# Attention rows as two 64-row matmuls, with heads regrouped at the load

## The chip, the cores and the metric

The kernel runs on one core of one Trainium2 chip. The metric is the device time of one execution in microseconds (us); the time before is the median of three runs. A profile is taken of one further execution, and its own time is given beside it.

## What is computed

A Nystrom attention with 32 landmarks per head is followed by a normalised MLP with a residual. There are 8 batches of 8 heads, 576 positions and 64 features per head.

```python
q_lm = q.reshape(B, H, 32, 18, D).mean(axis=3); k_lm = ...      # landmarks
A  = softmax(scale * q @ k_lm.T)      # 576 x 32 per head
Bm = softmax(scale * q_lm @ k_lm.T)   # 32 x 32
C  = softmax(scale * q_lm @ k.T)      # 32 x 576
Z  = Bm.T / (norms);  six times: Z = 2 * Z - Z @ Bm @ Z
attn = A @ Z @ C @ v                  # per head
x  = attn with heads side by side     # 8 x 576 x 512
xn = (x - mean) / sqrt(var + 1e-6) * g_ln
out = x + relu(xn @ w_ch1) @ w_ch2    # 512 -> 2048 -> 512
```

## The kernel before

**Units.** Four heads make a unit `u`, so a batch has two units (`U` = 2). Within a unit the four heads' 32 landmarks fill the 128 partitions. Batches 0 and 1 are handled one by one by `attention(b)`; batches 2 to 7 by `attention2` in four sets: (2), (3, 4), (5, 6) and (7).

**Loads.** All loads stand in one queue, that of SP, in program order. Batches 0 and 1 use `load` (L80), one copy of 128 partitions per tensor and unit. Batches 2 to 7 use `load_seg` (L100): k and q and the even v units are one copy of 128 rows of 4608 bytes (576 KB as the profile counts it). The odd v units are `turned`: two copies of 64 rows with the halves exchanged. Tiles come from the pool `stage` with six buffers, so a load waits until POOL has cast the tile loaded six places before it. SP's queue also holds the stores of results (`store`, L749) and the transposing copies of `xn` into `xnT` (L732).

**Casts and landmarks.** `Coming` (L497) holds the parts of a set in the order k, q, v and hands out loads, casts and jobs; `prepare` (L917) calls it between steps. POOL casts each load to fp16 (`nat`, `natv`) and, for most q tiles, adds up the 18 rows of a landmark (`asum`, `s`). DVE transposes the tiles (`xT`) and finishes the landmarks (`lmk`, `lmq`).

**Rows.** `rows_of` (L467) makes one block of at most 128 output positions at a time. Per unit it multiplies `ea` (the unit's exponentials, 128 landmark rows by up to 128 positions) with `zcbd`, a block-diagonal 128 x 260 tile: four heads of 64 columns plus four mask columns that give the sum of each softmax. The products go to `psy`, in one bank per unit, DVE takes reciprocals (`rcpd`) and scales (`xblk`). `zcbd` is made by one masked DVE product per unit.

**MLP stream.** `mlp()` is a generator of matmuls in nine groups of four blocks: `psh` (first layer, needs the four `xnT` blocks of the group), then `pso` (second layer). `fill(n)` puts n of its steps into TensorE's queue between the steps of the attention. The order on every engine is thus fixed when the program is built. `hT` (ACT) and `ot` (DVE) empty the three banks of the pool `psM`, which `psh`, `pso`, the transposes and dummy tiles share. In groups 2 and later the `xnT` blocks come by the transposing copies.

**Prologue.** `warm(n, cols)` issues dummy matmuls on zeros into a `psM` tile named `idle`. `turn_tile` transposes tiles of batches 0 and 1 on TensorE, `sums` adds landmarks up there.

**Exchange of halves.** In `scores` and in the products of `attention2` the odd unit of a pair uses column positions shifted by 64, so that its results come out with exchanged halves. Before, v of odd units is loaded exchanged to fit, and a second mask `mask4t` serves these units.

Of the kernel before, what the change touches and what calls it, by code (L numbers as in the profile page):

```python
# [9 lines left out]
FP16 = mybir.dt.float16  # L10
FP32 = mybir.dt.float32
UINT32 = mybir.dt.uint32
AF = mybir.ActivationFunctionType
ALU = mybir.AluOpType
AX = mybir.AxisListType

P = 128
# [3 lines left out]
def kernel(  # L21
# [10 lines left out]
    nc = tc.nc  # L32

    B, H, S, D = q.shape
# [5 lines left out]
    SEG = S // LM  # L40
    KCH = DM // P
    MCH = HID // P
    U = H // 4
    NJ = 9
# [7 lines left out]
        name=nc.get_next_instruction_name(), act_func_set_id=6, ins=[], outs=[]))  # L52

    const = ctx.enter_context(tc.tile_pool(name="const", bufs=1))
# [5 lines left out]
    keep = tc.keep_in_program_order  # L60
# [8 lines left out]
    dve, pool, scalar = Ordered(nc.vector), Ordered(nc.gpsimd), Ordered(nc.scalar)  # L69
    act = scalar.activation  # L70

    def MM(o, l, r, rb=0, cb=0, start=True, stop=True, skip=False):
        keep(nc.tensor.matmul(o, l, r, start=start, stop=stop, tile_position=(rb, cb),  # L73
                              skip_group_check=(skip or cb != 0)))
# [5 lines left out]
    def load(src, b, u, queue):  # L80
        t = stage.tile([P, 2, NJ, D], FP32, name="stg", tag="stg")
        keep(queue.dma_start(
            out=t[:],
            in_=src[b, 4 * u:4 * u + 4].rearrange("(r e) (t j) d -> (e t) r j d", e=2, j=NJ)))
        return t

    raw = {0: {}, 1: {}}
# [11 lines left out]

    def load_seg(src, b, u, queue, turned=False):  # L100
        t = stage.tile([P, SEG, D], FP32, name="stg", tag="stg")
        rows = src[b, 4 * u:4 * u + 4].rearrange("h (l j) d -> (h l) j d", j=SEG)
        for o, i_ in ((0, 64), (64, 0)) if turned else ((0, 0),):
            n = 64 if turned else P
            keep(queue.dma_start(out=t[ds(o, n), :, :], in_=rows[ds(i_, n), :, :]))
        return t


# [34 lines left out]
    mask4 = const.tile([P, 4], FP32, name="mask4")  # L143
# [10 lines left out]
                            base=63, pattern=[[64, 2]], channel_multiplier=-1)  # L154


    mask4t = const.tile([P, 4], FP32, name="mask4t")
    nc.gpsimd.tensor_copy(out=mask4t[:, 0:2], in_=mask4[:, 2:4])
    nc.gpsimd.tensor_copy(out=mask4t[:, 2:4], in_=mask4[:, 0:2])

    eps_ln = const.tile([P, 1], FP32, name="eps_ln")
    nc.vector.memset(eps_ln[:], 1e-6)
# [3 lines left out]
    NZ = 6  # L166
    natv_buf = []
    for i in range(NV):
        t = const.tile([P, H // 2, NJ, D + 1], FP16, name=f"natv{i}")
        nc.gpsimd.memset(t[:, :, :, D:D + 1], 1.0)  # L170
        natv_buf.append(t)
    zcbd_buf = []
    for i in range(NZ):
        zcbd_buf.append(const.tile([P, 4 * (D + 1)], FP16, name=f"zcbd{i}"))

    def zc_of(i):
        return zcbd_buf[i][:, ds(4 if i % 2 == 0 else 0, 4 * D)].rearrange("p (h d) -> p h d", d=D)

    cast_v(0)
    bones = const.tile([P, 4, 32], FP16, name="bones")
    for u in range(U):
        for nm in ("q", "k"):
            cast_qk(0, u, nm, dve)
        if u == 0:

            dve.tensor_copy(out=bones[:], in_=mask4[:, :, None].broadcast_to([P, 4, 32]))
            for i, t in enumerate(zcbd_buf):
                dve.tensor_copy(out=t[:, ds(0 if i % 2 == 0 else 4 * D, 4)],  # L190
                                in_=(mask4t if i in (3, 5) else mask4)[:])


    load_qk(1)
# [54 lines left out]
    def warm(n, cols):  # L249
        idle = psM.tile([P, 512], FP32, name="idle", tag="pm")  # L250
        for _ in range(n):
            MM(idle[:, 0:cols], zeros[:, 0:P], zeros[:, 0:cols])
# [27 lines left out]
    def turn_tile(b, w, nm):  # L280
        i = 0 if nm == "q" else 1
        if b == 1:
            if not i and w == 0:
                pss = ps1.tile([P, 2, U, 64], FP32, name="pss", tag="p1")
                nat_pss[b, 0], nat_pss[b, 1] = pss[:, 0, :, :], pss[:, 1, :, :]
            turn_part(w, nm, 0)
            turn_part(w, nm, 1)
            return None
        if w == 0:
            nat_pss[b, i] = psM.tile([P, U, 64], FP32, name="pss" + nm, tag="pm")  # L290
        n16 = nat_tiles[b, nm, w]
        t = aprep.tile([P, NJ, P], FP16, name="xT", tag="xT" + nm, bufs=5 if nm == "q" else 4)
        early_xT[b, nm, w] = t
        last = (w, i) == (U - 1, 1)
        pst = ps2.tile([P, NJ, P], FP16, name="pst", tag="p2")
        if last:
            sums(b, w, i, n16)
        for j in range(NJ):
            TR(pst[:, j, :], n16[:, j, :, :].rearrange("p r d -> p (r d)"), ident16[:])
        if not last:  # L300
            scalar.copy(t[:], pst[:])
            sums(b, w, i, n16)
        return t, pst

    def attention(b):
        W, first = U, b == 0
# [5 lines left out]
        def p2(shape, dtype, name):  # L312
# [4 lines left out]
            out=qbd[:],  # L317
            in0=nat_pss[b, 0][:].rearrange("p u (e l) -> p (u e) l", e=2)[:, :, None, :]
            .broadcast_to([P, W * 2, 2, LM]),
            in1=mask2[:, None, :, None].broadcast_to([P, W * 2, 2, LM]), op=ALU.mult)  # L320
# [8 lines left out]
        for w in range(W):  # L329
            for h in range(4):  # L330
                r, e = divmod(h, 2)
# [8 lines left out]
        for w in range(W):  # L340
# [5 lines left out]
            t = aexp.tile([P, NJ, 64], FP16, name="ect", tag="e")  # L346
# [7 lines left out]
        ea = []  # L354
# [52 lines left out]
        pszc = p1([P, W, D], "pszc")  # L407
        for w in range(W):
            for h in range(4):
                sl = ds(32 * h, 32)  # L410
                MM(pszc[sl, w, :], st[sl, w, LM:], cv[sl, w, :], rb=32 * h, cb=32 * h)
        zcbd = []
        for w in range(W):
            dve.tensor_tensor(
                out=zc_of(w), in0=pszc[:, w, None, :].broadcast_to([P, 4, D]),
                in1=mask4[:, :, None].broadcast_to([P, 4, D]), op=ALU.mult)
            zcbd.append(zcbd_buf[w])
        yield "zc"

        yield from rows_of((b,), ea, zcbd)  # L420

    def softmax_of(psb, W):
        rsum = asm.tile([P, W], FP32, name="rsum", tag="rsum")
# [41 lines left out]


    def rows_of(bs, ea, zcbd):  # L467
        for i, b in enumerate(bs):
            t0 = 0
            while t0 < S:  # L470
                j, pb = divmod(b * S + t0, P)
                n = min(P - pb, S - t0)
                rows = ds(pb, n)
                xb = x_of(j)
                psy = ps2.tile([P, U * 512], FP32, name="psy", tag="p2")
                for u in range(U):
                    MM(psy[rows, ds(508 - 256 if u == 0 else 512, 4 * (D + 1))],
                       ea[U * i + u][:, ds(t0, n)], zcbd[U * i + u][:], cb=pb)
                rcpd = asm.tile([P, U * 4], FP32, name="rcpd", tag="rcpd")
                dve.reciprocal(  # L480
                    out=rcpd[rows, :].rearrange("s (u h) -> s u h", u=U),
                    in_=psy[rows, ds(252, 520)].rearrange("s (a x) -> s a x", x=4)[:, 0::129, :])
                if pb == 0:
                    rowsum[j] = mstat.tile([P, 1], FP32, name="rowsum", tag="rowsum")
                dve.scalar_tensor_tensor(
                    out=xb[rows, :].rearrange("s (h e) -> s h e", e=D),
                    in0=psy[rows, ds(256, 512)].rearrange("s (h e) -> s h e", e=D), scalar=1.0,
                    in1=rcpd[rows, :, None].broadcast_to([n, 8, D]),
                    op0=ALU.mult, op1=ALU.mult, accum_out=rowsum[j][rows, :])
                t0 += n  # L490
                if pb + n == P:
                    block_done(j)
                yield "rows"
# [3 lines left out]
    class Coming:  # L497
# [28 lines left out]
        def load(self, i, queue=nc.sync):  # L526
            nm, w = self.parts[i]
            b, u = self.units[w]
            self.stg[i] = load_seg({"q": q, "k": k, "v": v}[nm], b, u, queue,
                                   turned=(nm == "v" and u % 2 == 1))  # L530


        def cast(self, i):
# [66 lines left out]
    def attention2(bs, c):  # L600
# [63 lines left out]
                    ea.append(e)  # L664
            yield
        pszc = ps2.tile([P, 2, 512], FP32, name="pszc", tag="p2")
        zcbd = []
        for w in range(W):
            for h in range(4):
                sl = ds(32 * h, 32)  # L670
                cb = 32 * ((h + 2 * (w % 2)) % 4)
                MM(pszc[ds(cb, 32), w % 2, ds(D * (w // 2), D)], st[sl, w, LM:], cv[sl, w, :],
                   rb=32 * h, cb=cb)
        for w in range(W):
            dve.tensor_tensor(
                out=zc_of(2 + w),
                in0=pszc[:, w % 2, None, ds(D * (w // 2), D)].broadcast_to([P, 4, D]),
                in1=(mask4t if w % 2 else mask4)[:, :, None].broadcast_to([P, 4, D]),
                op=ALU.mult)
            zcbd.append(zcbd_buf[2 + w])  # L680
        yield

        yield from rows_of(bs, ea, zcbd)

    ln_ready = {0}
    rowsum, variances, rstds, xn_of = {}, {}, {}, {}
# [165 lines left out]
    def fill(n):  # L852
        for _ in range(n):
            if not next(stream, False):
                return
# [8 lines left out]
    for w, nm in [(w, nm) for w in range(U) for nm in ("q", "k")]:  # L864
        last_tile = turn_tile(0, w, nm)
        if (w, nm) == (1, "q"):
            next(a0)
        warm(2, 384)
    next(a0)
    warm(1, 512)  # L870
    next(a0)
    warm(1, 512)
    scaled_by_pe()
# [14 lines left out]
    turn_tile(1, 1, "q")  # L888
    sums(1, 0, 0, nat_tiles[1, "q", 0])
    sums(1, 0, 1, nat_tiles[1, "k", 0])  # L890
    warm(1, 384)
    load_v(1)
    fill(1)
    turn_tile(1, 1, "k")
    sums(1, 1, 0, nat_tiles[1, "q", 1])
    fill(1)
    next(a0)
    warm(1, 256)
    fill(2)
    next(a0)  # L900
    fill(4)
# [95 lines left out]
```

## Time and profile before

| | |
|---|---|
| median of 3 runs | 329.57 us (328.02 to 329.58) |
| the profiled execution's own time | 330.85 us |
| its span, first to last instruction | 329.1 us |
| mean TensorE clock granted | 0.992 |
| TensorE busy | 315.4 us in 3668 matmuls |
| HBM read | 36.70 MB |

The page gives busy time by engine, then the span in 40 slices of 8.2 us (a digit is tenths busy, and a line gives the GB/s moved by the 16 DMA engines), then the chain of work that ended last, then groups of instructions and DMA issues with their time to landing. A timeline line reads: start, length, engine, code line, operation, written tile <- read tiles, rows*columns of the array used, shape, count, and in brackets the idle time before and who ended it. The end of a matmul is modelled, so distances between starts say more than lengths. A line of a stretch gives for each engine the busy us and the count, then the mean clock, the DMA engines' mean busy share and GB/s.

### The profile page before, as it was taken

The page shows a single profiled execution, that of the slowest core. Times are in us where ns is not written, and L with a number is a line of the kernel's source. Part 1 is how long each engine was busy: PE and PEld are TensorE (multiplying, and loading weights), DVE is VectorE, ACT ScalarE, POOL GpSimd, SP SyncE. Part 2 cuts the span into 40 slices and gives each one's busy share as a digit, 9 for nine tenths or more (in the row PEclk, how much of TensorE's full clock was granted, in tenths as well). Part 3 has the DMA queues.
Part 4 walks back from the last instruction along what each step waited for, and adds up shares of the span by engine and source line. Part 5 has one row for each costly group of instructions (what it writes and reads, how often), then busy time and mean ns, then how long its engine had stood idle before and what let it go on. Part 6 is the DMA issues. An engine that isn't in the chain of part 4 may idle for free.

```text
span 329.1 us, 8722 instructions
## 1 busy us (share of the span) xinstructions
PE 315.4 (96%) x3668; PEld 160.1 (49%) x3668; DVE 142.3 (43%) x368; ACT 149.3 (45%) x295; POOL 125.4 (38%) x193
## 2 busy tenths in 40 slices
PE   8789999799978999999999999999999999999994
PEld 8557755344433444544544454544444444444443
DVE  2667239767972368767142356411441120010012
ACT  3376853367630572586214574463068107305600
POOL 2489879958899651397400022100043000000000
PEclk9999999799999999999999999999999999999998
DMA  7999999879997696541024022320241124032023
GB/s 278 394 385 385 386 405 270 323 229 244 327 236 268 165 336 198 112 100 33 4 66 83 16 35 64 82 50 2 64 97 32 32 64 98 0 75 57 0 55 72
DMA packets 34095, 50.37 MB, mean 153 GB/s; under 512 B 17540, under 2 KB 17800, under 8 KB 34056
## 3 DMA queue, kind: packets, MB, share of 16 engines
q1 hardware_dynamic: 34056, 49.82, 52.1%
q8 instruction: 28, 0.46, 0.6%
q14 instruction: 11, 0.09, 0.1%
HBM read 36.70 MB, written 9.44 MB: 140 GB/s over the span
## 4 chain that ended last, share of the span: by engine, by line
PE 89%; DVE 4%; DMA 2%; ACT 1%; issue 1%; SPq 0%
PE psh L73 39%; PE pso L73 37%; PE pscv L73 3%; PE psy L73 3%; DMA stg<-in_k_dram 2%; PE psn L73 2%; DVE xblk L67 1%; ACT xT L67 1%; PE psec L73 1%; PE psea L73 1%; DVE xT L67 1%; DVE lmk L67 1%; DVE ot L67 1%; PE idle L73 0%; PE psb L73 0%
## 5 line engine op out<-in xcount | busy, mean ns | idle before, releaser
L73 PE MATMUL pso<-w,hT 128*128 128x512 f16 (+1 forms) x592 | 135.3, 376 | 0.0
L73 PE MATMUL psh<-xnT,w 128*128 128x512 f16 (+1 forms) x640 | 135.2, 358 | 0.1
L67 ACT ACTIVATE hT<-psh 128x512 f16<-128x512 f32 x144 | 84.6, 598 | 82.1 <-PE psh L73 81.6
L73 PEld LDWEIGHTS <-w 128*128 128x128 f16 x640 | 59.0, 98 | 56.3 <-issue 1.1
L73 PEld LDWEIGHTS <-hT 128*128 128x128 f16 x592 | 56.2, 98 | 58.0 <-issue 2.1
L67 DVE SCALAR_TENSOR_TENSOR ot<-pso,rstd,xblk 128x512 f32<-128x512 f32 (+1 forms) x37 | 27.1, 732 | 88.3 <-PE pso L73 87.9
L67 ACT ACTIVATE junk<-xblk,negm 128x512 f16<-128x512 f32 x36 | 26.0, 721 | 35.5 <-POOL negm L67 35.2
L67 POOL TENSOR_SCALAR negm<-rowsum 128x1 f32<-128x1 f32 x28 | 5.3, 190 | 94.2 <-DVE xblk L67 93.2
L67 POOL CAST nat<-stg 128x1152 f16<-128x1152 f32 x28 | 31.5, 1144 | 6.7 <-DMA stg<-in_q_dram 5.2
L67 DVE SCALAR_TENSOR_TENSOR xblk<-psy,rcpd 128x512 f32<-128x512 f32 (+1 forms) x40 | 27.6, 691 | 2.2
L67 DVE SCALAR_TENSOR_TENSOR st<-st,psn 128x128 f16<-128x128 f16 (+2 forms) x36 | 11.3, 315 | 30.6 <-PE psn L73 30.5
L67 POOL CAST natv<-stg 128x1152 f16<-128x1152 f32 x16 | 18.1, 1147 | 12.9 <-DMA stg<-in_v_dram 10.3
L67 DVE STREAM_TRANSPOSE xT<-nat 128x576 uint32<-128x576 uint32 x24 | 18.4, 767 | 6.1 <-PE psea L73 6.1
L67 POOL TENSOR_SCALAR xn<-xblk,negm 128x512 f16<-128x512 f32 x28 | 19.1, 692 | 0.8
L73 PE MATMUL psy<-zcbd,ea 128*128 128x260 f16 (+1 forms) x80 | 15.6, 276 | 0.6 <-DVE zcbd L67 0.5
L67 DVE TENSOR_REDUCE lmk<-xT 128x64 f16<-128x1152 f16 x12 | 16.1, 1342 | 0.0
L67 POOL TENSOR_TENSOR asum<-asum 128x256 f32<-128x256 f32 (+2 forms) x30 | 15.0, 500 | 2.4
L67 DVE RECIPROCAL rcpd<-psy 128x8 f32<-128x8 f32 (+1 forms) x40 | 8.0, 201 | 17.1 <-PE psy L73 16.9
L67 ACT ACTIVATE ea<-psea 128x576 f16<-128x576 f32 x12 | 7.1, 647 | 15.4 <-PE psea L73 15.4
L67 POOL TENSOR_TENSOR asum<-nat 128x576 f32<-128x576 f16 x10 | 12.8, 1276 | 0.8
L73 PEld LDWEIGHTS <-st 32*32 32x32 f16 x448 | 5.6, 89 | 15.3 <-issue 9.5
L73 PE MATMUL pscv<-natv,ecT 32*32 32x65 f16 x864 | 9.8, 195 | 3.0 <-issue 3.0
(98 smaller groups left out, 205.0 us busy)
## 6 DMA issues: line engine op xcount, KB each, us to landing
stg<-in_q_dram SPq DMA_DIRECT2D x16, 576.0 KB, 7.0
stg<-in_k_dram SPq DMA_DIRECT2D x16, 576.0 KB, 8.5
out_dram<-ot SPq DMA_DIRECT2D x70, 128.0 KB, 2.3
wstg<-in_moe_w_ch_dram SPq DMA_DIRECT2D x16, 512.0 KB, 6.9
stg<-in_v_dram SPq DMA_DIRECT2D x10, 576.0 KB, 6.6
stg<-in_v_dram SPq DMA_DIRECT2D x12, 288.0 KB, 8.9
xnT<-xn SPq DMA_TRANSPOSE x28, 2.7
out_dram<-ot SPq DMA_DIRECT2D x4, 64.0 KB, 2.0
```

Source lines behind the costliest of these rows:

```text
L67: return lambda *args, **kw: keep(getattr(self.engine, op)(*args, **kw))
L73: keep(nc.tensor.matmul(o, l, r, start=start, stop=stop, tile_position=(rb, cb), skip_group_check=(skip or cb != 0)))
```

## The change

Heads are regrouped: unit `u` now holds heads 2u, 2u+1, 4+2u and 5+2u, so that the lower 64 partitions belong to heads of the first half of the row and the upper 64 to the second half. `load` keeps one copy of 128 partitions. `load_seg` always makes two copies of 64 partitions; the exchange moves from v to q and k of odd units. The rows matmul of each unit is split into two with 64 rows of the array each: half `f` of both units goes to one bank. `zcbd` becomes one tile per batch with two heads per partition half (130 columns), made by one masked product for both units. In the prologue some dummy matmuls go and one turn moves behind other work.

```diff
 def load(src, b, u, queue):
-        in_=src[b, 4 * u:4 * u + 4].rearrange("(r e) (t j) d -> (e t) r j d", e=2, j=NJ)))
+        in_=src[b].rearrange("(r w e) (t j) d -> w (e t) r j d", r=2, e=2, j=NJ)[u]))
 def load_seg(src, b, u, queue, turned=False):
     t = stage.tile([P, SEG, D], FP32, name="stg", tag="stg")
-    rows = src[b, 4 * u:4 * u + 4].rearrange("h (l j) d -> (h l) j d", j=SEG)
-    for o, i_ in ((0, 64), (64, 0)) if turned else ((0, 0),):
-        n = 64 if turned else P
-        keep(queue.dma_start(out=t[ds(o, n), :, :], in_=rows[ds(i_, n), :, :]))
+    rows = src[b].rearrange("(r w e) (l j) d -> w r (e l) j d", r=2, e=2, j=SEG)[u]
+    for half in range(2):
+        keep(queue.dma_start(out=t[ts(half, 64), :, :], in_=rows[half ^ turned]))
...
-    mask4t = const.tile([P, 4], FP32, name="mask4t")
-    nc.gpsimd.tensor_copy(out=mask4t[:, 0:2], in_=mask4[:, 2:4])
-    nc.gpsimd.tensor_copy(out=mask4t[:, 2:4], in_=mask4[:, 0:2])
+    masks = const.tile([P, 2], FP32, name="masks")
+    nc.gpsimd.tensor_tensor(out=masks[:], in0=mask4[:, 0:2], in1=mask4[:, 2:4], op=ALU.add)
...
-        zcbd_buf.append(const.tile([P, 4 * (D + 1)], FP16, name=f"zcbd{i}"))
+    zcbd_buf = [const.tile([P, 2, 2, D + 1], FP16, name=f"zcbd{i}") for i in range(NZ // 2)]
...
-            for i, t in enumerate(zcbd_buf):
-                dve.tensor_copy(out=t[:, ds(0 if i % 2 == 0 else 4 * D, 4)],
-                                in_=(mask4t if i in (3, 5) else mask4)[:])
+            for t in zcbd_buf:
+                dve.tensor_copy(out=t[:, :, :, D],
+                                in_=masks[:, None, :].broadcast_to([P, 2, 2]))
...
-        for w in range(W):
-            dve.tensor_tensor(
-                out=zc_of(w), in0=pszc[:, w, None, :].broadcast_to([P, 4, D]),
-                in1=mask4[:, :, None].broadcast_to([P, 4, D]), op=ALU.mult)
+        masked(zcbd_buf[0], pszc[:])
+    def masked(out, zc):
+        dve.tensor_tensor(out=out[:, :, :, 0:D], in0=zc[:, :, None, :].broadcast_to([P, 2, 2, D]),
+                          in1=masks[:, None, :, None].broadcast_to([P, 2, 2, D]), op=ALU.mult)
...
 def rows_of(bs, ea, zcbd):
+    first = 512 - 4 * (D + 1)
     for u in range(U):
-        MM(psy[rows, ds(508 - 256 if u == 0 else 512, 4 * (D + 1))],
-           ea[U * i + u][:, ds(t0, n)], zcbd[U * i + u][:], cb=pb)
+        for f in range(2):
+            half = ts(f, 64)
+            MM(psy[rows, ds(first + 2 * (D + 1) * (2 * f + u), 2 * (D + 1))],
+               ea[U * i + u][half, ds(t0, n)],
+               zcbd[i][half, u, :, :].rearrange("p a e -> p (a e)"), rb=64 * f, cb=pb)
...
-                               turned=(nm == "v" and u % 2 == 1))
+                               turned=int(nm != "v" and u % 2 == 1))
...
-        warm(2, 384)
+        if (w, nm) != (U - 1, "k"):
+            warm(2, 384)
     next(a0)
-    warm(1, 512)
...
-    warm(1, 384)
     load_v(1)
     fill(1)
-    turn_tile(1, 1, "k")
     sums(1, 1, 0, nat_tiles[1, "q", 1])
     fill(1)
+    turn_tile(1, 1, "k")
     next(a0)
-    warm(1, 256)
     fill(2)
```

In `attention2` the masked products of a pair of units become one in the same way. DVE reads `psy` at a stride of 65 for `rcpd` and `xblk`.

More of the change, by code (lines that the diff above doesn't have):

```diff
@@ L171 @@
         natv_buf.append(t)
-    zcbd_buf = []
-    for i in range(NZ):
-        zcbd_buf.append(const.tile([P, 4 * (D + 1)], FP16, name=f"zcbd{i}"))
-    def zc_of(i):
-        return zcbd_buf[i][:, ds(4 if i % 2 == 0 else 0, 4 * D)].rearrange("p (h d) -> p h d", d=D)
+    zcbd_buf = [const.tile([P, 2, 2, D + 1], FP16, name=f"zcbd{i}") for i in range(NZ // 2)]
     cast_v(0)
@@ L411, in attention @@
                 MM(pszc[sl, w, :], st[sl, w, LM:], cv[sl, w, :], rb=32 * h, cb=32 * h)
-        zcbd = []
-        for w in range(W):
-            dve.tensor_tensor(
-                out=zc_of(w), in0=pszc[:, w, None, :].broadcast_to([P, 4, D]),
-                in1=mask4[:, :, None].broadcast_to([P, 4, D]), op=ALU.mult)
-            zcbd.append(zcbd_buf[w])
+        masked(zcbd_buf[0], pszc[:])
         yield "zc"
-        yield from rows_of((b,), ea, zcbd)
+        yield from rows_of((b,), ea, zcbd_buf[0:1])
+    def masked(out, zc):
+        dve.tensor_tensor(out=out[:, :, :, 0:D], in0=zc[:, :, None, :].broadcast_to([P, 2, 2, D]),
+                          in1=masks[:, None, :, None].broadcast_to([P, 2, 2, D]), op=ALU.mult)
     def softmax_of(psb, W):
@@ L476, in rows_of @@
                 for u in range(U):
-                    MM(psy[rows, ds(508 - 256 if u == 0 else 512, 4 * (D + 1))],
-                       ea[U * i + u][:, ds(t0, n)], zcbd[U * i + u][:], cb=pb)
+                    for f in range(2):
+                        half = ts(f, 64)
+                        MM(psy[rows, ds(first + 2 * (D + 1) * (2 * f + u), 2 * (D + 1))],
+                           ea[U * i + u][half, ds(t0, n)],
+                           zcbd[i][half, u, :, :].rearrange("p a e -> p (a e)"),
+                           rb=64 * f, cb=pb)
+                heads = psy[rows, ds(first, 8 * (D + 1))].rearrange("s (h x) -> s h x", x=D + 1)
                 rcpd = asm.tile([P, U * 4], FP32, name="rcpd", tag="rcpd")
-                dve.reciprocal(
-                    out=rcpd[rows, :].rearrange("s (u h) -> s u h", u=U),
-                    in_=psy[rows, ds(252, 520)].rearrange("s (a x) -> s a x", x=4)[:, 0::129, :])
+                dve.reciprocal(out=rcpd[rows, :], in_=heads[:, :, D])
                 if pb == 0:
@@ L486, in rows_of @@
                     out=xb[rows, :].rearrange("s (h e) -> s h e", e=D),
-                    in0=psy[rows, ds(256, 512)].rearrange("s (h e) -> s h e", e=D), scalar=1.0,
+                    in0=heads[:, :, 0:D], scalar=1.0,
                     in1=rcpd[rows, :, None].broadcast_to([n, 8, D]),
@@ L666, in attention2 @@
         pszc = ps2.tile([P, 2, 512], FP32, name="pszc", tag="p2")
-        zcbd = []
         for w in range(W):
@@ L673, in attention2 @@
                    rb=32 * h, cb=cb)
[L674 to L680, printed above, removed]
+        for y in range(W // 2):
+            masked(zcbd_buf[1 + y], pszc[:, :, ts(y, D)])
         yield
-        yield from rows_of(bs, ea, zcbd)
+        yield from rows_of(bs, ea, zcbd_buf[1:])
     ln_ready = {0}
```

## The prediction

> **What bounds the kernel now.** I read the page's shares and chain first, then its DMA rows, then busy time by stretch, then TensorE's timeline at the places where something else could end last.
>
> ```profile
> PE 315.4 (96%) x3668; PEld 160.1 (49%) x3668; DVE 142.3 (43%) x368; ACT 149.3 (45%) x295; POOL 125.4 (38%) x193
> ...
> DMA  7999999879997696541024022320241124032023
> GB/s 278 394 385 385 386 405 270 323 229 244 327 236 268 165 336 198 112 100 33 4 66 83 16 35 64 82 50 2 64 97 32 32 64 98 0 75 57 0 55 72
> ...
> PE 89%; DVE 4%; DMA 2%; ACT 1%; issue 1%; SPq 0%
> ...
> stg<-in_v_dram SPq DMA_DIRECT2D x10, 576.0 KB, 6.6
> stg<-in_v_dram SPq DMA_DIRECT2D x12, 288.0 KB, 8.9
> ```
>
> TensorE carries 89% of the chain. But for the first 130 us (16 slices of 8.2 us) the DMA engines are nearly full too, and a 288 KB load takes longer to land than a 576 KB one. The stretches say why:
>
> ```profile
> core 0: us, PE busy (x) PEld busy (x) DVE busy (x) ACT busy (x) POOL busy (x), PEclk, DMA share, GB/s
> 44.00:49.00 5.00, 5.00 (x70) 2.49 (x69) 2.54 (x9) 1.28 (x3) 3.70 (x5) 1.00 1.02 410
> 50.00:55.00 5.00, 5.00 (x30) 2.66 (x29) 4.85 (x13) 1.44 (x2) 4.52 (x8) 1.00 1.03 228
> 77.00:80.00 3.00, 3.00 (x30) 1.17 (x28) 2.40 (x5) 2.29 (x7) 2.69 (x6) 1.00 0.99 218
> 116.00:119.00 3.00, 3.00 (x60) 1.42 (x58) 2.94 (x6) 2.60 (x6) 2.09 (x3) 1.00 1.04 230
> 120.00:126.00 6.00, 6.00 (x88) 2.63 (x88) 4.26 (x9) 3.55 (x7) 1.59 (x2) 1.00 1.02 409
> ```
>
> The engines are busy all the time (share 1.0), yet move 410 GB/s while whole 128-row loads pass and 218 to 230 while the `turned` v loads pass, which are two copies of 64 rows each.
>
> ```profile
> 46.55 0.81 PE L73 MATMUL pso<-w,hT 128*128 128x512 f16 x3
> 47.29 0.41 PE L73 MATMUL psy<-zcbd,ea 128*64 128x260 f16 x2
> 47.63 1.47 PE L73 MATMUL pso<-w,hT 128*128 128x512 f16 x6
> 48.94 0.39 PE L73 MATMUL psy<-zcbd,ea 128*128 128x260 f16 x2
> 49.16 0.59 PE L73 MATMUL pso<-w,hT 128*128 128x512 f16 x2
> ...
> 59.44 0.22 PE L73 MATMUL psb<-lmk,lmq 32*32 32x32 f16 x8 [1.67 <-DVE lmq L67]
> ...
> 106.40 0.81 PE L73 MATMUL psh<-xnT,w 128*128 128x512 f16 x3
> ...
> 141.00 0.38 PE L73 MATMUL psh<-xnT,w 128*128 128x512 f16 x1
> ```
>
> A full-array rows step costs 0.22 us (48.94 to 49.16), with no gap: six `pso` at 0.216 from 47.63 end at 48.93. A step in 64 columns costs 0.43: `pso` ends at 46.55 + 3 x 0.216 = 47.20 and resumes at 47.63. Two places wait on loads: 59.44, where TensorE waits for q's landmarks, and the starts of MLP groups 2 and 3 (106.40, 141.00), which need the four transposed `xnT` blocks. Those transposes stand in SP's queue behind the loads.
>
> [...] The trace agrees for column tiles (0.09 us in, about 0.10 out). It has no fp16 tile of 64 rows by 128 columns; the nearest, the one 4-row by 128-column product (`psg`, 13.22), starts 0.10 after the 512-column product ahead of it (12.90 + 0.22) has streamed. [...] The trace agrees after the wait at 59.44: the mean clock from 60 to 71 us is 0.84, 0.16 x 11 = 1.7 us of work lost.
>
> **Loads.** `load_seg` now issues two 64-row copies for every k, q and v unit of batches 2 to 7: 36 loads, of which 6 were split before. SP issues 30 more copies at 0.33 to 0.58 us, at most 17 us over 85; SP's waits for buffers (12.6 us on `natv`, 6.5 on `nat`) and for stores (99.9 on `ot`) cover that. The data path has none. A load is 590 kB: at 410 GB/s 1.44 us, at 226 (mean of 228, 218, 230) 2.61, so 1.17 more. Batches 0 and 1 (`load`) keep 128 rows and 2304-byte runs: nothing.
>
> I follow the queue in SP's order. The first such load (issued 38.84, landing 7.0 later) moves from 44.4. Six stage buffers keep up to 16 us of loads in flight, more than POOL's longest job (cast 1.14 and sums 3.6), so I take the queue as never empty.
> - Set 0 (batch 2): k lands at 47.0, 49.6, q at 52.2, 54.8. POOL casts and sums the first q until 52.2 + 4.7 = 56.9, the second until about 61.6. Before, that was 58.1 and DVE's last `lmq` started at 59.97. TensorE's wait at 59.44 grows by about 1.7.
> - Group 2 needs `xnT` of block 11. Ahead of it: 24 loads (62.6), four blocks of stores (0.65 each by bytes: 2.6), four transposes (estimate 1.2 each from SP's median issue 1.23: 4.8). 44.4 + 70.0 = 114.4, against 106.40: TensorE 8.0 late. On the way DVE's in-order queue blocks: its transpose of the first k of the next set (the 19th load) ran at 93.48, and that k now lands at about 98. Behind it on DVE stand `st`, `ecT` and `ot`; `ot` frees the `psM` banks that the next `pso` products want. This wait is part of the 8.0, not beside it.
> - Group 3 needs block 15: all 36 loads (94.0), ten blocks of stores (6.5), eight transposes (9.6): 154.5, landing about 155. TensorE would be there at 114.4 + 34.6 + 1.7 (cold clock) = 150.7. It starts **14.0 late**.
> - Afterwards nothing is loaded and TensorE is dense. The wait just ended costs one cold window: **+1.7**.
>
> **Rows on TensorE.** 32 full steps: two pairs of 130 columns at about 0.06 each if the halves overlap, plus 0.09 in, 0.10 out and 0.01 for the first weights: 0.32 instead of 0.22, +0.10 each. Eight 64-row steps already pay the switch: 0.43 to 0.33. In all +3.2 - 0.8 = +2.4. Unmeasured, so bounded: no drain for row tiles gives -0.10 x 40 = -4.0; halves that don't overlap 0.21 x 32 = +6.7. I take the drain, since every other mode change in the trace pays it. What falls before group 3 hides in the waits above; after it lie 12 full steps and three 64-row ones: +1.2 - 0.3 = **+0.9** (-1.5 to +2.5).
>
> **Mask products.** 16 DVE products of 0.42 become 8: 3.4 us of DVE, which idles 87.9 us on `pso` anyway. Only in the prologue does TensorE wait for the second (psy at 20.27): -0.4. Reads of `psy` at stride 65 have no row; I keep 0.69 us, and a tenth more on four steps between 49 and 59 would be 0.3, inside the wait.
>
> **Prologue order.** Dummy products of 1920 columns go (0.8 us, partly in waits), and they held `psM` buffers; k's turn moves behind block 1's transposes, so `psh` at 25.39 comes up to 0.9 earlier, until POOL's weight casts (0.69 each, the twelfth done at 29.79) meet it: about -0.5. Three small fills (0.15 each) and one POOL copy go, under input landings up to 9.8. All of this is lost again in the longer wait at 59. The clock could drop without the dummies: at most 1.7, hidden likewise. 160 more TensorE instructions less 10 shift the two "issue" pauses of the chain (1.66 and 1.34): -3 to +3, before group 2, hidden too.
>
> **Sum.** 14.0 + 1.7 + 0.9 = 16.6. The profiled execution is 330.85 (span 329.1), so 347.4; it stands 1.3 above the median of 329.57, hence **346.1**.
>
> **Rivals.** *A, the loads stay hidden:* engines fall out of step, so that one half's tail and the next half's head use both sides. At 2.2 us a load block 15 lands near 140 and block 11 near 105: nothing waits but 59.44. Then +2.4 rows, +0.6 wait, -0.9 prologue: about 332 (330 to 335). For it: the page's 8.9 us is a latency. Against it: in all three stretches the rate stayed near half for as long as halves were in flight, also beside whole loads (50 to 55). *B, faster:* a row tile of full width needs no drain; rows give -4.0, prologue -0.9: 325. It decides only if the switch costs under 0.05 us each way and a load takes under 2.2 us; the place is each `psy` step between two `pso` or `psh` products. For it: a row tile leaves all columns in use. Against it: `psg` above, and the load rates. *C, the change doesn't do what it says:* the two halves' products run one after another. Rows then cost +6.7, of which 12 x 0.21 = 2.5 after group 3 shows: 348.
>
> **Chances and range.** Forecast with C 0.83, A 0.11 (a third within 0.5%), B 0.06. Within 0.5% (1.6 us) is about what a measurement of this kernel can't tell from no change. Faster 0.06, same 0.04, slower 0.90. At 2.4 us a load the sum is +9 (338); at 2.9 (what 590 kB takes at 203, a tenth below the lowest stretch shown) +27 (357). The range takes these and A's upper edge: 334 to 357.
>
> **What would show it.** Right: the load rows read 288 KB throughout; GB/s near 225 to about 150 us; `psh` groups 2 and 3 start near 114 and 155 after idle TensorE; `lmq` later at 59; a rows step of 0.32. Wrong: GB/s over 300 with only halves in flight, group 3 starting by 143, or `psy` steps of 0.12.

## The result, and the profile after

| | before | after |
|---|---|---|
| median | 329.57 us (328.02 to 329.67, 4 runs) | 347.94 us (345.07 to 348.48, 4 runs) |
| ratio | | 1.055 (95% interval 1.049 to 1.062) |
| the profiled execution's own time, its span | 330.85, 329.1 us | 347.65, 345.9 us |
| mean TensorE clock granted | 0.992 | 0.975 |

The changed kernel is 18 us slower; 346.1 was forecast. The lines of its page that answer to those shown of before:

```profile
PE 321.1 (93%) x3743; PEld 155.5 (45%) x3743; DVE 140.5 (41%) x357; ACT 150.0 (43%) x295; POOL 126.0 (36%) x192
...
DMA  7999999999999999993012302250124034022022
GB/s 275 391 387 385 373 229 239 261 292 213 213 208 162 281 205 213 220 214 67 2 28 56 75 17 45 63 83 12 32 64 87 2 83 99 2 61 62 2 56 68
...
PE 75%; DMA 12%; POOL 7%; issue 3%; SPq 1%; DVE 1%; ACT 0%; POOLq 0%
...
stg<-in_k_dram SPq DMA_DIRECT2D x24, 288.0 KB, 10.6
stg<-in_q_dram SPq DMA_DIRECT2D x24, 288.0 KB, 9.9
stg<-in_v_dram SPq DMA_DIRECT2D x24, 288.0 KB, 8.3
```

The DMA digits are 9 up to slice 18 (155 us; before up to about 130), while the rate falls from 373 to 229 GB/s in slice 6, from 43 us, where the first halved loads arrive, and then lies between 162 and 292, mostly near 215, to the end of the loads. TensorE's share of the chain fell from 89% to 75%, and DMA took 12%. All 72 copies of batches 2 to 7 are of 288 KB now. TensorE's timeline at the places that the prediction named:

```profile
62.16 0.22 PE L73 MATMUL psb<-lmk,lmq 32*32 32x32 f16 x8 [1.25 <-DVE lmq L67]
63.34 0.21 PE L73 MATMUL psb<-lmk,lmq 32*32 32x32 f16 x6 [0.96 <-DVE lmq L67]
...
110.40 0.42 PE L73 MATMUL pscv<-natv,ecT 32*32 32x65 f16 x31 [5.44 <-issue]
110.75 4.06 PE L73 MATMUL pso<-w,hT 128*128 128x512 f16 x11
114.65 0.81 PE L73 MATMUL psh<-xnT,w 128*128 128x512 f16 x3
...
154.66 0.47 PE L73 MATMUL psh<-xnT,w 128*128 128x512 f16 x1 [2.08 <-DMA xnT<-xn]
```

Group 2 starts at 114.65 (before 106.40), but nothing at its start waits for `xnT`: the wait is 5.44 us of "issue" (time in which the engine waited for nothing that the profile shows) ahead of 110.40, in the middle of 72 equal products, and the 11 `pso` after it take 3.90 us where 2.38 would do (0.216 each). Group 3 starts at 154.66 and does wait for the transposing copy. By stretches (the last three columns are clock, DMA share and GB/s):

```profile
core 0: us, PE busy (x) PEld busy (x) DVE busy (x) ACT busy (x) POOL busy (x), PEclk, DMA share, GB/s
50.00:55.00 5.00, 5.00 (x32) 1.89 (x32) 3.88 (x12) 1.44 (x2) 2.30 (x2) 1.00 1.03 236
85.00:95.00 10.00, 10.00 (x61) 3.89 (x58) 9.70 (x24) 5.01 (x10) 9.01 (x15) 1.00 1.04 219
107.00:114.00 7.00, 3.60 (x39) 1.44 (x40) 0.00 (x0) 0.00 (x0) 6.60 (x10) 0.51 1.15 195
155.00:158.00 3.00, 3.00 (x11) 0.87 (x10) 0.91 (x3) 1.11 (x3) 1.33 (x3) 0.50 0.68 147
```

In the stretch over the first wait the clock is 0.51 on average, after the second 0.50: half.

### The profile page after: what moved, and what is told of

It is laid out like the page before. It is cut to its first block, busy times and chain, and to the rows that moved or that the text cites. A ratio compares the mean times of both kernels' runs of the same rounds, so it can differ in the third digit from the quotient of the medians.

```text
span 345.9 us, 8904 instructions
## 1 busy us (share of the span) xinstructions
PE 321.1 (93%) x3743; PEld 155.5 (45%) x3743; DVE 140.5 (41%) x357; ACT 150.0 (43%) x295; POOL 126.0 (36%) x192
## 4 chain that ended last, share of the span: by engine, by line
PE 75%; DMA 12%; POOL 7%; issue 3%; SPq 1%; DVE 1%; ACT 0%; POOLq 0%
PE psh L73 34%; PE pso L73 33%; DMA wstg<-in_moe_w_ch_dram 4%; POOL w L67 4%; DMA stg<-in_q_dram 3%; PE pscv L73 2%; DMA stg<-in_v_dram 2%; PE psy L73 2%; POOL asum L67 2%; PE psn L73 1%; DMA xnT<-xn 1%; POOL natv L67 1%; PE psea L73 1%; PE psec L73 1%; POOL nat L67 1%
## 5 line engine op out<-in xcount | busy, mean ns | idle before, releaser
L73 PE MATMUL psh<-xnT,w 128*128 128x512 f16 (+1 forms) x640 | 136.8, 361 | 2.3 <-DMA xnT<-xn 2.1
L73 PEld LDWEIGHTS <-hT 128*128 128x128 f16 x592 | 54.5, 98 | 59.8 <-issue 1.9
L73 PEld LDWEIGHTS <-ea 64*128 64x128 f16 (+1 forms) x160 | 4.9, 97 | 18.5 <-issue 14.1
```

## The experiments

Each experiment is named for the kernel that it starts from: those called after_ edit the changed kernel, those called before_ the kernel before; rows_only edits the changed kernel too. The starts of the MLP groups (from the timelines of the profiled executions), as differences to before, show where each kernel loses its time. A profiled execution need not lie at its kernel's median: that of before took 330.85 us, 1.3 above it, that of before_halves 341.22, 1.7 below, so the table is for the places of the losses and the medians for their sizes.

| us later than before | group 1 | group 2 | group 3 | last product |
|---|---|---|---|---|
| changed kernel | +4.0 | +8.3 | +13.7 | +16.3 |
| before_halves | +3.0 | +9.9 | +9.9 | +9.9 |
| before_far | +3.6 | +8.7 | +11.1 | +11.1 |
| after_near | +4.0 | +10.5 | +15.0 | +16.0 |
| before_halves_pad | +3.3 | +10.2 | +11.8 | +11.9 |
| after_pad | +2.5 | +7.0 | +10.7 | +11.8 |
| after_whole | -1.1 | -3.7 | -3.2 | -2.2 |
| before_even_odd | -0.6 | -3.4 | -3.5 | -3.5 |

### before_halves: the loads alone

```diff
-        for o, i_ in ((0, 64), (64, 0)) if turned else ((0, 0),):
-            n = 64 if turned else P
-            keep(queue.dma_start(out=t[ds(o, n), :, :], in_=rows[ds(i_, n), :, :]))
+        for o, i_ in ((0, 64), (64, 0)) if turned else ((0, 0), (64, 64)):
+            keep(queue.dma_start(out=t[ds(o, 64), :, :], in_=rows[ds(i_, 64), :, :]))
```

> The kernel before with one edit: every load of batches 2 to 7 is two 64-row copies, of the same heads into the same places. Theory 'loads' (the halved loads cost nearly all of the +18): GB/s near 220 until about 150 us, psh group 2 starts 7 to 8 us late (113 to 115), group 3 about 13 to 14 late (154 to 155), one cold clock after it; time 343 to 347. Theory 'rows' (the 64-row products and their mode switches cost it): 329 to 331. Theory 'prologue' (the clock lost at 15 to 22 us and what follows from it): 329 to 331.

Measured: 342.89 us, ratio 1.041 (1.036 to 1.046). By the medians the halved loads alone cost 13.6 of the 18 us. But the way there differs from the expectation, at least in the profiled execution, the fastest of the four: group 3 is 9.9 us late, not 13 to 14, and does not wait. There all is lost by group 2:

```profile
59.45 0.22 PE L73 MATMUL psb<-lmk,lmq 32*32 32x32 f16 x8 [1.68 <-DVE lmq L67]
62.31 0.21 PE L73 MATMUL psb<-lmk,lmq 32*32 32x32 f16 x4 [2.64 <-DVE lmq L67]
...
103.38 0.62 PE L73 MATMUL pscv<-natv,ecT 32*32 32x65 f16 x49 [3.86 <-issue]
103.93 5.45 PE L73 MATMUL pso<-w,hT 128*128 128x512 f16 x14
...
112.31 0.25 PE L73 MATMUL pscv<-natv,ecT 32*32 32x65 f16 x7 [2.32 <-issue]
112.50 3.94 PE L73 MATMUL pso<-w,hT 128*128 128x512 f16 x11
116.28 0.81 PE L73 MATMUL psh<-xnT,w 128*128 128x512 f16 x3
...
150.88 0.38 PE L73 MATMUL psh<-xnT,w 128*128 128x512 f16 x1
```

The same places of before:

```profile
60.19 0.21 PE L73 MATMUL psb<-lmk,lmq 32*32 32x32 f16 x6 [0.53 <-DVE lmq L67]
...
98.21 0.56 PE L73 MATMUL pscv<-natv,ecT 32*32 32x65 f16 x49 [1.66 <-issue]
98.70 3.19 PE L73 MATMUL pso<-w,hT 128*128 128x512 f16 x14
101.83 0.69 PE L73 MATMUL pscv<-natv,ecT 32*32 32x65 f16 x65
103.86 0.22 PE L73 MATMUL pscv<-natv,ecT 32*32 32x65 f16 x7 [1.34 <-issue]
104.01 2.55 PE L73 MATMUL pso<-w,hT 128*128 128x512 f16 x11
```

The last `lmq` comes later: the product that waits for it starts at 62.31 instead of 60.19. With the slower clock after it (0.69 on average from 60 to 71 us, before 0.84) group 1 is 3.0 late. The two pauses, 1.66 and 1.34 us before, are 3.86 and 2.32: +3.2. The `pso` after them take 5.38 us (14) and 3.78 (11), before 3.13 and 2.39: +3.6. 3.0 + 3.2 + 3.6 = 9.8, nearly the whole delay.

### after_whole and rows_only: everything but the halved loads

```diff
-        rows = src[b].rearrange("(r w e) (l j) d -> w r (e l) j d", r=2, e=2, j=SEG)[u]
-        for half in range(2):
-            keep(queue.dma_start(out=t[ts(half, 64), :, :], in_=rows[half ^ turned]))
+        rows = src[b, 4 * u:4 * u + 4].rearrange("h (l j) d -> (h l) j d", j=SEG)
+        keep(queue.dma_start(out=t[:], in_=rows))
```

> The changed kernel with one edit: every load of batches 2 to 7 is one 128-row copy of four neighbouring heads. The regrouping of heads and the exchange for odd units are left out by this, so heads are mixed up in the products; sizes and order of all work on the engines stay. Theory 'loads': GB/s near 400 again, psh group 3 starts by 145, time 331 to 334 (rows +2.4, prologue 0 to +1.8). Theory 'rows': 345 to 348. Theory 'prologue': 345 to 348.

> The changed kernel with 128-row loads as in after_whole (heads mixed up in the same way) and with the prologue of the kernel before: what is left of the change is the row-half products and the merged mask products. Theory 'loads': the rows cost +2.4 by 0.10 us in 32 steps and -0.10 in 8, less 0.4 for the mask product in the prologue: 331 to 332.5. Theory 'rows': 340 or more. Theory 'prologue' (its late start is all that after_whole has above before): 329 to 330.

The diff is that of after_whole; rows_only has it too, and the prologue of the kernel before.

Measured: after_whole 328.73 us, ratio 1.000 (0.998 to 1.003); rows_only 328.79, ratio 0.998 (0.996 to 1.000). The profiled execution of rows_only took 1724 us, its others 328 to 331, so no view of it is used. Without halved loads the whole loss is gone. Both are 2 to 5 us below what I expected. The trace of after_whole shows where the rows' price may have gone. From group 3 (137.82) to the last product (322.81) it takes 184.99 us, before 184.04 (141.00 to 325.04): the rows cost the +0.9 that was forecast for this part. But ahead of group 2 it has no "issue" pause above 0.5 us, where the profiled execution of before had 3.0. The price of the rows and a gain of that size cannot be told apart in a median.

### after_old_prologue and before_new_prologue: the prologue alone

after_old_prologue puts the `warm` calls and the turn of the kernel before back into the changed kernel; before_new_prologue does the reverse.

> The changed kernel with the prologue of the kernel before (dummy products and order of turns). Theory 'loads': psh starts at about 25.4 instead of 27.2, and the gain is lost again in the waits for the loads by group 3, whose queue does not depend on it: 347 to 349, no difference from the changed kernel beyond 0.5. Theory 'prologue': most of the +18 goes, 330 to 335. A third: the 1.8 us stay gained to the end, 345.5 to 346.5.

> The kernel before with the changed kernel's prologue alone (fewer dummy products, the last turn of block 1 later). Theory 'loads': nothing of the +18 is here: 328.5 to 331, at most +1.8 if the clock drops at 15 us and the later waits don't hide it. Theory 'prologue': 340 or more. My step in the prediction (-0.5, hidden): 329.

Measured: 348.82 us (ratio 1.060, 1.054 to 1.065) and 330.49 us (1.003, 1.000 to 1.006). With the loads in the way the prologue makes no difference that these runs show; alone it costs at most 0.6%. The stretch from 16 to 20 us of the changed kernel:

```profile
16.00:20.00 4.00, 4.00 (x92) 2.37 (x95) 1.57 (x7) 1.40 (x3) 2.69 (x3) 0.50 1.06 389
```

The same stretch of before_new_prologue:

```profile
16.00:20.00 4.00, 4.00 (x84) 2.20 (x73) 1.80 (x7) 2.04 (x4) 3.03 (x3) 0.65 1.05 389
```

The clock (third number from the end) drops in this stretch; before it was 1.00. But the missing dummies alone do not decide it: in after_whole and after_sp_act, with the same prologue, it stayed at 1.00 (in after_whole `psh` started 1.0 us earlier than before, not 1.8 later), and in after_old_prologue, which has the dummies, it was 0.57. What decides is not shown; one trace of each kernel cannot tell.

### before_even_odd: is it the halves, or the number of copies?

```diff
-        for o, i_ in ((0, 64), (64, 0)) if turned else ((0, 0),):
-            n = 64 if turned else P
-            keep(queue.dma_start(out=t[ds(o, n), :, :], in_=rows[ds(i_, n), :, :]))
+        for o, i_ in ((0, 64), (64, 0)) if turned else ((0, 0), (1, 1)):
+            if turned:
+                keep(queue.dma_start(out=t[ds(o, 64), :, :], in_=rows[ds(i_, 64), :, :]))
+            else:
+                keep(queue.dma_start(out=t[o::2, :, :], in_=rows[i_::2, :, :]))
```

> The kernel before, with every load of batches 2 to 7 that was one 128-row copy made by two copies of 64 rows, the even partitions and the odd ones, where before_halves took the lower and the upper 64. Same number, size and row length of copies as before_halves. [...] each copy now spans both halves, GB/s near 400 again, 328 to 331. Rival 'more and smaller copies' (36 more copies of 64 rows, whatever the partitions): as before_halves, 341 to 344.

Measured: 328.30 us, ratio 0.999 (0.997 to 1.001). (30 loads are split newly, so there are 30 more copies than before, not the 36 of the expectation; before_halves has the same number.) The stretch from 44 to 49 us of before_even_odd, where k and q of batch 2 arrive:

```profile
44.00:49.00 5.00, 4.69 (x68) 2.33 (x66) 3.03 (x9) 1.19 (x2) 4.08 (x4) 1.00 1.03 407
```

The same stretch of before_halves:

```profile
44.00:49.00 5.00, 5.00 (x70) 2.49 (x69) 2.44 (x9) 1.28 (x3) 1.89 (x3) 1.00 1.03 247
```

The same number of copies of the same size, with the same row length: 407 against 247 GB/s. What counts here is that a copy reaches both partition halves, not its size and not how many there are.

### after_sp_act: the two halves from two queues

```diff
-            keep(queue.dma_start(out=t[ts(half, 64), :, :], in_=rows[half ^ turned]))
+            keep((queue, nc.scalar)[half].dma_start(out=t[ts(half, 64), :, :], in_=rows[half ^ turned]))
```

> The changed kernel, the second 64-row copy of each load issued from ACT's queue instead of SP's. Theory 'one half at a time in one queue' (the rate is halved because copies of one queue pass one after another): both halves in flight together, GB/s over 350, psh group 3 by 146, 330 to 335 with up to 3 us for ACT's 36 issues and its waits for buffers. Theory 'halves serialize whatever the queue': GB/s near 220, 346 to 352.

Measured: 358.09 us, ratio 1.089 (1.085 to 1.094). The stretch from 44 to 49 us, and lines of the timelines of ACT and TensorE:

```profile
44.00:49.00 5.00, 0.00 (x0) 0.00 (x0) 0.00 (x0) 0.00 (x0) 1.32 (x2) 0.50 1.04 247
```

```profile
45.95 3.82 ACTq L104 DMA_DIRECT2D stg<-in_v_dram  x2
49.82 1.19 ACT L67 ACTIVATE ect<-psc 128x576 f16<-128x576 f32 x2 [17.23 <-DMA stg<-in_q_dram]
...
51.55 0.58 PE L73 MATMUL psh<-xnT,w 128*128 128x256 f16 x2 [15.62 <-ACT hT L67]
```

Copies of both queues had been issued since 38.7, and the rate is the 247 GB/s of before_halves. From 85 to 95 us it is 222 GB/s, against 219 in the changed kernel: the second queue brought no rate. The extra 10 us come with ACT's issues: its issues wait for load buffers, ACT computes nothing for 17.2 us, and TensorE stands 15.6 us for the `hT` behind them.

### after_near and before_far: five us more than before_halves

The changed kernel is 5 us above before_halves. Its 64-row copies are slower: between 76 and 105 us the first landings (the trace of the changed kernel has 3237 landing records for 203 copies, 16 for each but for a few; the first of each copy is taken) of two copies in a row lie 1.36 us apart (median), in before_halves 1.32. The two runs exchange the grouping of heads. after_near has `src[b, 4 * u:4 * u + 4]`, split into the same halves, in the changed kernel; before_far has the changed kernel's `load_seg` and its exchange on q and k in the kernel before.

> The changed kernel with one edit: the two 64-row copies of a load fetch four neighbouring heads (heads 4u to 4u+3) instead of the regrouped ones; the exchange for odd units stays. Heads land in other columns of the result by this. It asks where the 4.6 us are by which the changed kernel is above before_halves. Theory 'rows' (the row-half products and mode switches, hidden with whole loads by shorter pauses): 346.5 to 349, GB/s near 213 between 77 and 105 us as in the changed kernel. Theory 'grouping' (halves of regrouped heads come at 213 GB/s where halves of neighbours come at 233: 36 loads of 590 kB, 0.24 us each, 8 us at the end of the queue): 342 to 345, GB/s near 233, no wait for xnT at group 3.

> before_halves with the regrouped heads of the changed kernel in batches 2 to 7, the exchange on q and k (heads are mixed up in the products by this; the rows stay full-array products). Theory 'rows': as before_halves, 341 to 344. Theory 'grouping': 345 to 348, GB/s near 213 between 77 and 105 us and group 3 waits for xnT until about 154.

Measured: after_near 348.69 us, ratio 1.060 (1.055 to 1.064); before_far 343.22, ratio 1.045 (1.040 to 1.049). "Grouping" falls as the cause of the five us: they stay with the kernel whose rows are split. (Copies in before_far do come 1.35 us apart, but its time is that of before_halves.) That spoke for "rows". But 64-row matmuls are no evident reason for slower copies, and the two kernels differ in one thing more: where their buffers lie.

### after_pad, before_halves_pad, before_pad64: the place of the buffers

```diff
+    pad = const.tile([P, 8], FP32, name="pad")
+    nc.gpsimd.memset(pad[:], 0.0)
     NV = 2
```

before_pad64 has `[P, 16]` in place of `[P, 8]`. The places are worked out from the sizes of the tiles in the programs; no trace shows an address.

> The changed kernel with an unused tile of 32 bytes per partition ahead of all later tiles (and its memset). The change made the mask and zcbd tiles 1632 bytes smaller, so the six load buffers start at 62688 instead of 64320: 32 bytes past a multiple of 64, where the kernel before has a multiple of 64. The pad puts them at 62720. In the changed kernel a 64-row copy takes 1.36 us in dense stretches, in before_halves 1.31 and 1.26. Theory 'place': copies at 1.26 to 1.31 again, group 3 no longer waits for xnT, 342.5 to 345. Theory 'rows' (the 5 us above before_halves come from TensorE's own work): 347 to 349, copies still 1.36.

> before_halves with the same 32-byte pad, which moves its load buffers off the multiple of 64 (to 64352). Theory 'place': copies take 1.35, the queue ends 3 us later, 345.5 to 348. Theory 'rows': as before_halves, 341.5 to 344.

> The kernel before with an unused tile of 64 bytes per partition ahead of the later tiles, so that its load buffers start at 64384, a multiple of 128, instead of 64320. In after_pad (62720, a multiple of 128) the loads between 16 and 40 us, all of 128 rows, came at 404 GB/s; in the eight other kernels so far, with buffers 32, 64 or 96 past a multiple of 128, at 386 or 387. Theory 'place': 404 GB/s here too; the weights and first loads are through about 1 us earlier, TensorE then bounds the end, so 327.5 to 329.3, and it beats the kernel before only if the starts of the MLP are set by those loads. Rival 'something else of the changed kernel': 386 GB/s, 329 to 330.

| kernel | buffers start at | past a multiple of 64, 256 | us between copies, 76 to 105 us | GB/s, 16 to 40 us | median us | ratio |
|---|---|---|---|---|---|---|
| before_halves | 64320 | 0, 64 | 1.32 | 386 | 342.89 | 1.036 to 1.046 |
| before_halves_pad | 64352 | 32, 96 | 1.37 | 387 | 343.08 | 1.037 to 1.051 |
| changed kernel | 62688 | 32, 224 | 1.36 | 386 | 347.94 | 1.049 to 1.062 |
| after_pad | 62720 | 0, 0 | 1.33 | 404 | 342.24 | 1.036 to 1.047 |
| before_pad64 | 64384 | 0, 128 | | 387 | 328.76 | 0.997 to 1.002 |

32 unused bytes took 5.7 us off the changed kernel, by the medians. So the split rows alone do not make the five us; nor does the place alone, for before_halves_pad has the worse place and the time of before_halves. In both pairs of halved kernels a 64-row copy takes 3 to 4% longer off the multiple of 64. In after_pad the whole loads ahead of them gain too. The stretch from 16 to 40 us of the changed kernel:

```profile
16.00:40.00 24.00, 22.16 (x379) 16.14 (x378) 12.96 (x45) 15.54 (x29) 20.93 (x25) 0.88 1.05 386
```

The same stretch of after_pad:

```profile
16.00:40.00 24.00, 22.07 (x371) 15.99 (x364) 12.93 (x45) 15.62 (x29) 21.86 (x26) 0.88 1.05 404
```

And the start of group 3 in after_pad, with its wait for the transposing copy (151.74 instead of 154.66):

```profile
151.74 0.38 PE L73 MATMUL psh<-xnT,w 128*128 128x512 f16 x1 [1.69 <-DMA xnT<-xn]
```

In the profiled executions the two kernels are 4.5 us apart at the last product. Of these, 2.9 are there by group 3, for block 15's `xnT` lands that much earlier (151.7 against 154.6). That is about what the copies give: 72 of them at 0.035 us are 2.5 us, and 24 us at 404 instead of 386 GB/s are 1.1. The other 1.5 follow group 3: after the wait there the clock stood at half in the changed kernel, and at 1.00 in after_pad (151 to 157 us).

That the place was the cause is tested in the changed kernel alone. In the other pair the slower copies came too, with a wait of 1.30 us at group 3, and the profiled executions are 2.0 us apart, but the medians hardly differ (343.08 against 342.89). The pad moves every tile behind it, not the load buffers alone. before_far, with the buffers of before_halves, has copies 1.35 apart, so the place is not all that sets their pace. The changed kernel and after_pad were not run side by side, and not all runs were on one chip; but kernels of one kind agree across runs (changed kernel, after_near and after_old_prologue 347.9 to 348.8; before_halves, before_far and before_halves_pad 342.9 to 343.2). The split rows themselves show as 1.0 to 1.1 us after group 3 in all kernels of the table that have them. The rest of what places and rows do together stays open.

before_pad64 refutes my reason for the 404 GB/s: a multiple of 128 does not give it. Of the 13 kernels whose profiles are used only after_pad has buffers at a multiple of 256, and only it shows 404. The difference is 4.7% (404 against 386); that the place makes it is not shown by one kernel.

None of the runs beats the kernel before: the best, before_even_odd and before_pad64, are equal to it within their intervals.

## Why the prediction was right, and where it was not

- **Loads: right.** 2.61 us per halved load was forecast from 226 GB/s; two copies 1.36 us apart are 2.72. The queue was never empty to 155 us. before_halves (13.6 us of the 18) and after_whole (none of them left) show that this term carries the result. Rival A falls: the rate stays near 215 GB/s to the end of the loads, so no overlap of one half's tail with the next half's head shows. (203 GB/s, named for the upper edge of the range, is a tenth below the mean of 226, not below the lowest stretch, 218; nothing hangs on it.)
- **Set 0: right wait, too small.** POOL was to be done with the second q at about 61.6, 1.7 us after the 59.97 at which the last `lmq` had started. That `lmq` did wait for POOL (in before_halves DVE idles 1.99 us for it), but came at 62.05 in before_halves and at 63.07 in the changed kernel, 2.1 and 3.1 later; group 1 starts 3.0 and 4.0 late.
- **Group 2: right number, wrong cause.** 114.4 was worked out as the landing of block 11. In the changed kernel that copy landed at 113.3, so it would have held TensorE to about there; what did hold it was the pause of 5.44 us at 110.40 and the clock after it. In before_halves block 11 landed at 110.4 and `psh` started at 116.28. The step that failed is the last of the paragraph on prologue order: I let the two "issue" pauses shift by -3 to +3 and called them hidden. They grew with the loads and were on the path: 4.0 by group 1, 2.4 more of pause (5.44 against 3.00) and 1.5 more in the 11 `pso` after it make 7.9 of the 8.3. The wait on DVE that I put into the 8.0 did not come: DVE turned that k at 97.97, as forecast, but TensorE has no wait of 0.2 us or more between 67 us and this pause.
- **Group 3: right for this placement only.** 155 against 154.66, and the wait for `xnT` is there (2.08 us). But the profiled execution of before_halves, with the same loads, had no wait and lost 9.9 us by then instead of 14, and after_pad 10.7. In before_halves block 15 landed at 149.2 although two copies took 2.63 us in the dense stretch, as forecast: the sum was some 5 us too large, and which of its terms is not shown. In the changed kernel, where every later buffer had moved by 1632 bytes with the smaller tiles, slower copies made up for that: luck.
- **Cold clock after group 3: right here, but not certain.** +1.7 forecast; from group 3 to group 4 the delay grows from 13.7 to 15.2. The same loss after the pause ahead of 110.40 (1.5 us) was missing from the sum. The clock fell in the pause of 5.44 us (0.51 from 107 to 114 us), after waits of 1.67 and 0.53 us in before (0.84 from 60 to 71 us) and after that of 2.08 in the changed kernel (0.50 from 155 to 158 us). But it stayed at 1.00 after the pauses of 1.66 and 1.34 us in before (98 to 106 us), and in after_near, where the wait at group 3 was longer, 2.49 us (155 to 160 us):

```profile
155.98 0.38 PE L73 MATMUL psh<-xnT,w 128*128 128x512 f16 x1 [2.49 <-DMA xnT<-xn]
```

  So the length of a wait alone does not tell whether the clock falls, and the one fall after a wait in the trace of before was too little to count on +1.7.

- **Rows: right.** A full step was forecast at 0.32:

```profile
50.35 1.47 PE L73 MATMUL pso<-w,hT 128*128 128x512 f16 x6
51.75 0.29 PE L73 MATMUL psy<-zcbd,ea 64*128 64x130 f16 x4
51.97 0.39 PE L73 MATMUL pso<-w,hT 128*128 128x512 f16 x1
```

  Six `pso` end at 50.35 + 1.30 = 51.65, `psy` starts 0.10 later, and `pso` resumes at 51.97: 0.32 in all. Four products of 130 columns start within 0.07, so the two halves overlap, and rival C falls; the drain that rival B denied, 0.10 us ahead of `psy`, is there. After group 3 the rows cost 1.1 in the changed kernel and 1.0 in after_whole, against +0.9.
- **Prologue: wrong sign, no matter.** -0.5 forecast for `psh` at 25.39; it started at 27.19, after the clock had dropped. In after_old_prologue it started at 26.20, and the time is no shorter, so the start is hidden by later waits. The -0.4 for the mask products did not come either: the first `psy` waits 0.54 us for `zcbd`, before 0.53.

The sum of 16.6 meets the measured 16.3 on TensorE partly by luck. The pauses and the size of the early loss were wrong, but in the changed kernel the queue's end, which set group 3, covers both; and that end met its forecast only through the slower copies.

## What to carry to other kernels

Before a load is cut in two, look at which partitions each piece reaches: two pieces that each span both halves cost nothing here (407 GB/s from 44 to 49 us), two that each fill one half came at 247 GB/s and cost 13.6 us. Follow a slower load not only to the data it brings but to everything behind it in the DMA engines, and price the slower clock that may come after each new wait (1.5 us after the pause ahead of 110.40 in the changed kernel; after the 2.49 us in after_near it stayed at 1.00). When a change makes a constant smaller, see where the later buffers come to lie: 32 unused bytes took 5.7 us off the changed kernel, though they left the time of before_halves as it was (343.08 against 342.89).

## What the runs showed of the hardware

- **TensorE's "issue" pauses were longer in the kernels with the higher DMA share.** The "issue" pauses come at the same two instructions of TensorE's stream (numbers 2753 and 3009 of its products and weight loads in the trace, 256 apart) in before and before_halves, at 3009 in the changed kernel. In these three each ends 2.4 to 3.6 us after a packet of the DMA queue that the page calls "instruction" starts (29 packets, 0.48 MB in the changed kernel). The longest pause was 5.4 us in the changed kernel (DMA share 1.07 from 95 to 105 us), 3.9 in before_halves (1.06), 1.7 in before (0.97), 0.3 in before_even_odd (0.76), and no longer than 0.5 in after_whole (0.68). That the packet is held up by the data ahead of it is an estimate from this order, not shown: no run changed that alone.
- **32 bytes can matter.** With load buffers 32 bytes off a multiple of 64, by the sizes of the tiles, 64-row copies were 3 to 4% slower in two pairs of kernels (1.36 us against 1.33, 1.37 against 1.32); in a third kernel (before_far) they were about as slow, 1.35, without that.
- **Whole loads at 404 GB/s** in the one kernel with buffers at a multiple of 256, against 386 or 387 in the twelve others. No second kernel tests it.
